# High halves of q and k copied on GpSimd, and the bias of the exponential computed on ScalarE

## The chip, the cores and the metric

The kernel runs on one core of one Trainium2 chip. The metric is the time of one execution on the device in microseconds. A core has five engines that run beside each other, each with its own queue in program order: TensorE (PE in the profile; its weight loads are PEld), VectorE (DVE), ScalarE (ACT), GpSimd (POOL) and SyncE (SP, which here only issues DMAs). An instruction waits at the head of its engine's queue until what it needs is there, and everything behind it on that engine waits too.

## The reference

Attention within clusters, followed by a two-layer network. Each query and key is assigned to the nearest of 16 centroids, and a query attends only to keys of its own cluster:

```
q_assign = argmax(einsum('bhsd,hcd->bhsc', q_n, c_n), axis=-1)     # q_n, c_n: unit length
k_assign = argmax(einsum('bhsd,hcd->bhsc', k_n, c_n), axis=-1)
mask     = q_assign[:, :, :, None] == k_assign[:, :, None, :]
scores   = where(mask, q @ k.T / sqrt(D), -1e9)
attn     = softmax(scores)                                         # with 1e-9 added to the sum
x        = attn @ v                                                # heads joined: 3072 x 512
out      = (s * relu(x @ w_in)**2 + b) @ w_out
```

There are 4 batches, 8 heads, 768 positions, 64 values a head; w_in is 512 x 2048 and w_out 2048 x 512, all float32.

## The kernel before, in words

Every float32 factor of a large product is split in two float16 parts, a high half (the rounded value) and a low half (the rest), and three of the four products of halves are summed.

**Units and steps.** The attention is cut into 192 units, one for each batch, third of the positions, pair of heads, tile of 128 queries and head. The main loop (L699) has one iteration i for each unit. In it stand the scores of unit i (L455: four matmuls of 384 columns into a PSUM tile `sc`, of which there are two), the row maximum on VectorE (`maxima`, L464, which writes the negated maximum into column 0 of a small tile `ssm`), and the exponential (`exps`): L471 computes the bias, maximum times scale plus 14 ln 2, into column 1 of `ssm`, and L474 is the exponential on ScalarE, which reads `sc` and writes `p`. Then `high` (L119: `ph`, the high half of `p`, on ScalarE), `low` (L497: the low half on GpSimd, and L499: a DMA transpose of both halves into `PT`), and four units later `values` (L516 to L518: `PT` times v into `px`, in a single PSUM bank that is shared with small products; L524 to L528 divide by the sums on VectorE).

**The network.** 21 iterations behind the scores runs the network, in 192 steps as well, each with one 128-wide slice of the hidden layer for 256 rows: L574 (12 matmuls into `h`, one bank), L581 (relu on ScalarE, `r`), L583 and L584 (squares, `g` and `r`), L589 (the low half of `g` on GpSimd) and L601 (6 matmuls into `acc`). L609 and L610 scale and write out 256 rows after every 16 steps.

**The weights.** Each of 32 weight tiles is loaded (`wst`), converted on ScalarE (L203, L205, L216), VectorE (L209, L210) and GpSimd (L223), and, when the largest values of all are known, split in halves (L267 on ScalarE, L269 on VectorE). This fills the first iterations.

**The preparation of k and q.** `prep_k` runs 16 times (batch and pair of heads), `prep_q` 24 times (batch, third of the positions, four heads). Both load a block (`kn`, `qn`), find its largest value, scale it and split it: L185 writes the high half on ScalarE and L187 the low half on VectorE. Both build two operands for the scores. For k, `ka` holds the high and the low half side by side, and `kb` the high half and, beside it, a code of the cluster; for q, `qa` holds the low and the high half and `qb` the high half and the code. So the high half stands in both: L325 copies it from `ka` to `kb`, 768 values a partition, and L375 from `qb` to `qa`, 512 values a partition, both on VectorE. The DMA transposes L329 (`KA`) and L379 (`QA`) follow. From `KA` and `QA` TensorE computes the products with the centroids (`pk`, `pq`), VectorE turns them into the code (L288 to L294), and L342 and L392 transpose `kb` and `qb` into `KB` and `QB`. After the first batch there is one `kb` buffer: the copy into it waits until the preceding `KB` transpose has read it. The preparation of a block of q is begun 10 iterations before the first unit that uses it.

**What sets the order.** The program text is not the order of the queues. A scheduler orders every queue from the dependencies and from its own estimates of times; the helpers `behind` and `first_of_all` and the list `last_split` (the last instruction that wrote a half) only bound it at the start. So a change of three lines can reorder all queues.

Of the kernel before, what the change touches and what calls it, by code (L numbers as in the profile page):

```python
# [10 lines left out]
F32 = mybir.dt.float32  # L11
I32 = mybir.dt.int32
U32 = mybir.dt.uint32
AF = mybir.ActivationFunctionType
ALU = mybir.AluOpType
# [3 lines left out]
P = 128  # L19
# [7 lines left out]
def tile_cluster_attention_mlp(ctx, tc, q, k, v, cent, w_in, w_out, s_in, b_in, out):  # L27
# [12 lines left out]
    V = nc.vector  # L40
    G = nc.gpsimd
    A = nc.scalar
# [13 lines left out]
    def const(shape, dt, name):  # L56
        return cp.tile(shape, dt, tag=name, name=name)
# [17 lines left out]
    last_split = [None, None]  # L75
# [97 lines left out]
    bias = []  # L173
# [4 lines left out]
    def split(hi, lo, src, f, early):  # L178
        if early:
            A.activation(src, src, AF.Copy, scale=f)  # L180
            last_split[1] = A.activation(hi, src, AF.Copy)
            yield
            G.tensor_tensor(lo, src, hi, op=ALU.subtract)
        else:
            last_split[1] = A.activation(hi, src, AF.Copy, scale=f)  # L185
            yield
            V.scalar_tensor_tensor(lo, src, f, hi, op0=ALU.mult, op1=ALU.subtract)  # L187

    def fetch(p):
        ft = p // 2  # L190
# [110 lines left out]
    def prep_k(b, hp):  # L301
        kb = kb_kept
        if b == 0 and hp > 0:
            kb = sb.tile([P, 2 * T, P], F16, tag="big", name=f"kb_{hp}", bufs=BIGN).rearrange("p (h t) (e d) -> p h t e d", h=2, e=2)
# [6 lines left out]
        sm = [KSM[b][:, e, hp : hp + 1] for e in range(4)]  # L311
# [8 lines left out]
        if b == 0 and hp > 0:  # L320
            ka = sb.tile([P, 2 * T, P], F16, tag="big", name=f"ka_{hp}", bufs=BIGN).rearrange("p (h t) (e d) -> p h t e d", h=2, e=2)
        else:
            ka = sb.tile([P, 2, T, 2, D], F16, tag="big", name=f"ka_{n}", bufs=BIGN)
        yield from split(ka[:, :, :, 0, :], ka[:, :, :, 1, :], kn, sm[2], False)
        last_split[0] = V.tensor_copy(kb[:, :, :, 0, :], ka[:, :, :, 0, :])  # L325
        KA = sb.tile([P, 2 * T, P], F16, tag="KA", name=f"KA_{n}", bufs=5)
        KB = sb.tile([P, 2 * T, P], F16, tag="KB", name=f"KB_{n}", bufs=5)
        KS[(b, hp)] = (KA, KB)
# [15 lines left out]
    def prep_q(b, c, hq):  # L344
# [8 lines left out]
        sm = sb.tile([P, 4, 2], F32, tag="qsm", name=f"qsm_{n}", bufs=3)  # L353
# [6 lines left out]
        f = sm[:, 2, :]  # L360
# [4 lines left out]
        qa = sb.tile([P, 2 * T * P], F16, tag="big", name=f"qa_{n}", bufs=BIGN)[:, : nh * CT * 2 * D].rearrange("p (h t e d) -> p h t e d", h=nh, t=CT, e=2)  # L365
        qb = sb.tile([P, 2 * T * P], F16, tag="big", name=f"qb_{n}", bufs=BIGN)[:, : nh * CT * 2 * D].rearrange("p (h t e d) -> p h t e d", h=nh, t=CT, e=2)
        both = []
        for j in range(2):
            hs = slice(2 * j, 2 * j + 2)
            both.append(split(qb[:, hs, :, 0, :], qa[:, hs, :, 0, :], qn[:, hs], sm[:, 2, j : j + 1], b + c == 0))  # L370
        for z in zip(*both):
            yield
        for z in both:
            next(z, None)
        V.tensor_copy(qa[:, :, :, 1, :], qb[:, :, :, 0, :])  # L375
        QA = sb.tile([P, nh * CT, P], F16, tag="QA", name=f"QA_{n}", bufs=2)
        QB = sb.tile([P, nh * CT, P], F16, tag="QB", name=f"QB_{n}", bufs=2)
        QS[(b, c, hq)] = (QA, QB, sm)
# [55 lines left out]
                    yield  # L434


    LIFT = 14.0 * math.log(2.0)
    units = [(b, c, hp, t, h) for b in range(B) for c in range(NCH) for hp in range(NP) for t in range(CT) for h in range(2)]
    NU = len(units)
    U = {}  # L440
# [25 lines left out]
    def exps(i):  # L466
        j = i % 4
        sm = SM[i // 4]
        bi = sm[:, 1, j : j + 1]
        u = U[i]  # L470
        V.tensor_scalar(bi, sm[:, 0, j : j + 1], u["scale"], LIFT, op0=ALU.mult, op1=ALU.add)  # L471
        p = sb.tile([P, S], F32, tag="big", name=f"p_{i}", bufs=BIGN)
        total = {"accum_out": sm[:, 2, j : j + 1]} if i < RAW else {}
        last_exp[0] = A.activation(p.rearrange("p (a b) -> p a b", a=2), u["sc"], AF.Exp, bias=bi, scale=u["scale"], **total)  # L474
        u["p"] = p
# [284 lines left out]
```

## Time and profile before

| | |
|---|---|
| median of 3 runs | 1006.37 us (1002.96 to 1007.54) |
| the profiled execution | 1002.93 us |
| its span, first to last instruction | 1001.3 us |
| mean granted TensorE clock in the span | 0.932 of full speed |
| VectorE in L325, L375 and L471 | 15.6, 21.4 and 38.2 us |
| GpSimd's largest group, L497 | 310.3 us in 184 instructions |
| ScalarE's largest group, L474 | 188.4 us in 192 instructions |

How to read the lines below: a group of instructions has its line in the kernel, engine, operation, tile written <- tiles read, sizes and count, then its busy time in all, the mean of one in ns, and the idle time of the engine just before them with what ended it. The busy time of an engine counts overlapping instructions once. The "chain that ended last" is followed back from the last instruction, at each step to what released it or to its predecessor on the engine; its pieces are start, length, and what ran. A line "A <- B: total, times, longest" is the time for which A's engine sat idle until B was done.

### The profile page before, as it was taken

The page shows a single profiled execution, that of the slowest core. Times are in us where ns is not written, and L with a number is a line of the kernel's source. Part 1 is how long each engine was busy: PE and PEld are TensorE (multiplying, and loading weights), DVE is VectorE, ACT ScalarE, POOL GpSimd, SP SyncE. Part 2 cuts the span into 40 slices and gives each one's busy share as a digit, 9 for nine tenths or more (in the row PEclk, how much of TensorE's full clock was granted, in tenths as well). Part 3 has the DMA queues.
Part 4 walks back from the last instruction along what each step waited for, and adds up shares of the span by engine and source line. Part 5 has one row for each costly group of instructions (what it writes and reads, how often), then busy time and mean ns, then how long its engine had stood idle before and what let it go on. Part 6 is the DMA issues. An engine that isn't in the chain of part 4 may idle for free.

```text
span 1001.3 us, 22497 instructions
## 1 busy us (share of the span) xinstructions
PE 845.3 (84%) x8625; PEld 584.2 (58%) x8625; DVE 692.5 (69%) x1707; ACT 675.5 (67%) x1224; POOL 524.9 (52%) x502
## 2 busy tenths in 40 slices
PE   1568436977989899998899999997888998999997
PEld 1346224644566666665566776665666666767764
DVE  6797978889687756768877657687877665574100
ACT  3577666766477777766577877765777775778553
POOL 1225754555255666555466656643566664666422
PEclk9966656999999999999899999998999999999999
DMA  7875986686686976799898679987878776979300
GB/s 186 199 199 171 236 203 117 117 188 116 130 152 134 174 133 117 143 204 173 171 154 155 144 126 170 180 163 159 156 146 169 128 125 129 151 120 160 47 22 22
DMA packets 450299, 147.36 MB, mean 147 GB/s; under 512 B 417936, under 2 KB 446608, under 8 KB 450192
## 3 DMA queue, kind: packets, MB, share of 16 engines
q1 hardware_dynamic: 450192, 145.93, 74.8%
q8 instruction: 67, 1.10, 0.4%
q14 instruction: 40, 0.33, 0.1%
HBM read 35.69 MB, written 6.29 MB: 42 GB/s over the span
## 4 chain that ended last, share of the span: by engine, by line
PE 43%; DVE 19%; DMA 17%; ACT 8%; issue 5%; POOL 3%; SPq 1%; POOLq 0%; DVEq 0%; ACTq 0%
PE h L574 15%; PE acc L601 14%; PE sc L455 6%; DVE ssm L464 4%; DMA PT<-ph 3%; DMA QB<-qb 3%; DMA qn<-in_q_dram 2%; ACT p L474 2%; PE px L516 2%; PE px L518 2%; PE px L517 2%; DMA wst<-in_moe_w_out_dram 2%; DMA KB<-kb 2%; DMA kn<-in_k_dram 2%; POOL ph L497 2%
## 5 line engine op out<-in xcount | busy, mean ns | idle before, releaser
L497 POOL TENSOR_TENSOR ph<-p,ph 128x768 f16<-128x768 f32 x184 | 310.3, 1687 | 225.3 <-ACT ph L119 173.1
L574 PE MATMUL h<-x,wis 128*128 128x256 f16 x2304 | 295.7, 277 | 7.2 <-ACT r L581 2.9
L601 PE MATMUL acc<-wos,g 128*128 128x512 f16 x1152 | 297.4, 380 | 4.0 <-POOL g L589 3.6
L574 PEld LDWEIGHTS <-wis 128*128 128x128 f16 x2304 | 225.2, 99 | 66.0 <-issue 7.7
L474 ACT ACTIVATE p<-sc,ssm,qsm 128x768 f32<-128x768 f32 x192 | 188.4, 981 | 63.0 <-DVE ssm L471 37.2
L589 POOL TENSOR_TENSOR g<-r,g 128x256 f16<-128x256 f32 x192 | 137.2, 715 | 128.2 <-ACT r L584 117.7
L464 DVE TENSOR_REDUCE ssm<-sc 128x1 f32<-128x768 f32 x192 | 181.3, 949 | 24.9 <-PE sc L455 24.8
L581 ACT ACTIVATE r<-h,cf 128x256 f32<-128x256 f32 x192 | 90.0, 469 | 126.0 <-PE h L574 94.5
L601 PEld LDWEIGHTS <-g 128*128 128x128 f16 x1152 | 104.2, 98 | 86.1 <-POOL g L589 7.6
L119 ACT ACTIVATE ph<-p 128x768 f16<-128x768 f32 x174 | 144.8, 832 | 13.0 <-DMA PT<-ph 9.0
L516 PE MATMUL px<-vh,PT 128*128 128x65 f16 x1104 | 122.0, 198 | 22.7 <-DVE qsm L98 7.4
L455 PE MATMUL sc<-KA,QA 128*128 128x384 f16 x384 | 104.2, 351 | 32.9 <-ACT p L474 29.6
L517 PE MATMUL px<-vl,PT 128*128 128x64 f16 x1104 | 122.1, 195 | 0.0
L518 PE MATMUL px<-vh,PT 128*128 128x65 f16 x1104 | 121.6, 196 | 0.0
L517 PEld LDWEIGHTS <-PT 128*128 128x128 f16 x1104 | 105.3, 101 | 24.7 <-issue 16.4
L516 PEld LDWEIGHTS <-PT 128*128 128x128 f16 x1104 | 105.4, 100 | 23.3 <-issue 14.5
L455 PE MATMUL sc<-KB,QB 128*128 128x384 f16 x384 | 102.5, 352 | 17.9 <-DMA QB<-qb 16.1
L518 PEld LDWEIGHTS <-PT 128*128 128x128 f16 x1104 | 105.3, 100 | 3.1
L583 ACT ACTIVATE g<-r 128x256 f16<-128x256 f32 x192 | 79.4, 413 | 3.9
L584 ACT ACTIVATE r<-r 128x256 f32<-128x256 f32 x192 | 79.0, 412 | 3.6
L455 PEld LDWEIGHTS <-QA 128*128 128x128 f16 x384 | 37.2, 103 | 62.4 <-issue 37.4
L455 PEld LDWEIGHTS <-QB 128*128 128x128 f16 x384 | 38.4, 104 | 50.0 <-DMA QB<-qb 22.3
(152 smaller groups left out, 1031.8 us busy)
## 6 DMA issues: line engine op xcount, KB each, us to landing
wst<-in_moe_w_in_dram SPq DMA_DIRECT2D x16, 512.0 KB, 4.5
wst<-in_moe_w_out_dram SPq DMA_DIRECT2D x16, 512.0 KB, 4.0
kn<-in_k_dram SPq DMA_DIRECT2D x16, 384.0 KB, 3.8
qn<-in_q_dram SPq DMA_DIRECT2D x24, 256.0 KB, 3.8
vn<-in_v_dram SPq DMA_DIRECT2D x16, 384.0 KB, 4.1
out_dram<-o SPq DMA_DIRECT2D x12, 512.0 KB, 4.1
PT<-ph SPq DMA_TRANSPOSE x184, 4.0
x<-xn SPq DMA_TRANSPOSE x48, 2.8
```

Of the source, the lines that this page charges most:

```text
L119: A.activation(dst, src, AF.Copy)
L455: last_score[0] = nc.tensor.matmul(sc[:, e, :HALF], X[:, col, :], y[:, h * S + e * HALF : h * S + (e + 1) * HALF], start=st, stop=not st)
L464: last_max[0] = V.tensor_reduce(SM[i // 4][:, 0, j : j + 1], U[i]["sc"], axis=AX.XY, op=ALU.max, negate=True)
L474: last_exp[0] = A.activation(p.rearrange("p (a b) -> p a b", a=2), u["sc"], AF.Exp, bias=bi, scale=u["scale"], **total)
L497: G.tensor_tensor(u["ph"][:, 1, :], u["p"], u["ph"][:, 0, :], op=ALU.subtract)
L516: nc.tensor.matmul(o1, PT[:, kt, :], vh[:, h, kt, : D + 1], start=(kt == 0), stop=False)
L517: nc.tensor.matmul(o, PT[:, kt, :], vl[:, h, kt, :], start=False, stop=False)
L518: nc.tensor.matmul(o1, PT[:, T + kt, :], vh[:, h, kt, : D + 1], start=False, stop=(kt == T - 1))
L574: nc.tensor.matmul(ph[:, :CW], WSP[ft][0][:, wl, kt, :], XS[(b, c, kt)][:, :, xl, :], start=(i == 0), stop=(i == len(terms) - 1))
L581: A.activation(r, ph[:, :CW], AF.Relu, scale=MS[(b, c)][0])
L589: G.tensor_tensor(g[:, 1, :], r, g[:, 0, :], op=ALU.subtract)
L601: nc.tensor.matmul(acc[:, t, :], g[:, gl, rows], WSP[ft][1][:, wl, :], start=(ft == 0 and gl + wl == 0), stop=(ft == NF - 1 and gl == 1))
```

## The change

Three things. The copies L325 and L375 become GpSimd's. The bias of the exponential becomes an activation (Identity, with scale and bias read from memory) on ScalarE, in the queue that also holds the exponential; its constant is a tile `lift`, written once by GpSimd. And at the start, where the copy of k set `last_split[0]`, the low half of a split now sets it.

```
--- before.py
+++ after.py
@@ -184,7 +184,7 @@
         else:
             last_split[1] = A.activation(hi, src, AF.Copy, scale=f)
             yield
-            V.scalar_tensor_tensor(lo, src, f, hi, op0=ALU.mult, op1=ALU.subtract)
+            last_split[0] = V.scalar_tensor_tensor(lo, src, f, hi, op0=ALU.mult, op1=ALU.subtract)
 
     def fetch(p):
         ft = p // 2
@@ -322,7 +322,7 @@
         else:
             ka = sb.tile([P, 2, T, 2, D], F16, tag="big", name=f"ka_{n}", bufs=BIGN)
         yield from split(ka[:, :, :, 0, :], ka[:, :, :, 1, :], kn, sm[2], False)
-        last_split[0] = V.tensor_copy(kb[:, :, :, 0, :], ka[:, :, :, 0, :])
+        G.tensor_copy(kb[:, :, :, 0, :], ka[:, :, :, 0, :])
         KA = sb.tile([P, 2 * T, P], F16, tag="KA", name=f"KA_{n}", bufs=5)
         KB = sb.tile([P, 2 * T, P], F16, tag="KB", name=f"KB_{n}", bufs=5)
         KS[(b, hp)] = (KA, KB)
@@ -372,7 +372,7 @@
             yield
         for z in both:
             next(z, None)
-        V.tensor_copy(qa[:, :, :, 1, :], qb[:, :, :, 0, :])
+        G.tensor_copy(qa[:, :, :, 1, :], qb[:, :, :, 0, :])
         QA = sb.tile([P, nh * CT, P], F16, tag="QA", name=f"QA_{n}", bufs=2)
         QB = sb.tile([P, nh * CT, P], F16, tag="QB", name=f"QB_{n}", bufs=2)
         QS[(b, c, hq)] = (QA, QB, sm)
@@ -434,7 +434,8 @@
                     yield
 
 
-    LIFT = 14.0 * math.log(2.0)
+    lift = const([P, 1], F32, "lift")
+    G.memset(lift, 14.0 * math.log(2.0))
     units = [(b, c, hp, t, h) for b in range(B) for c in range(NCH) for hp in range(NP) for t in range(CT) for h in range(2)]
     NU = len(units)
     U = {}
@@ -468,7 +469,7 @@
         sm = SM[i // 4]
         bi = sm[:, 1, j : j + 1]
         u = U[i]
-        V.tensor_scalar(bi, sm[:, 0, j : j + 1], u["scale"], LIFT, op0=ALU.mult, op1=ALU.add)
+        A.activation(bi, sm[:, 0, j : j + 1], AF.Identity, scale=u["scale"], bias=lift)
         p = sb.tile([P, S], F32, tag="big", name=f"p_{i}", bufs=BIGN)
         total = {"accum_out": sm[:, 2, j : j + 1]} if i < RAW else {}
         last_exp[0] = A.activation(p.rearrange("p (a b) -> p a b", a=2), u["sc"], AF.Exp, bias=bi, scale=u["scale"], **total)
```

Lines behind L437 have moved by one: L472 below is the bias, L475 the exponential, L498 `ph` on GpSimd, L582, L584 and L585 are `r`, `g` and `r`, and L590 is `g` on GpSimd.

The scheduler orders the queues anew. SP's queue at the start, before: the first transposes of k (KA) and of the centroids (cT), loads, and the first transpose of q (QA).

```order
L329 DMA_TRANSPOSE KA_0_0_192<-ka_0_0_158 128x12x128
L329 DMA_TRANSPOSE KA_0_1_203<-ka_1_169 128x12x128
L160 DMA_TRANSPOSE cT_126<-cnat_120 128x3x128
L82 DMA vn_0_0_248<-in_v_dram 128x2x384
L125 DMA sv_250<-in_moe_s_dram 128x1
L125 DMA bv_252<-in_moe_b_dram 128x1
L379 DMA_TRANSPOSE QA_0_0_0_198<-qa_0_0_0_184 128x8x128
L82 DMA wst_0_255<-in_moe_w_in_dram 128x4x256
L82 DMA wst_1_258<-in_moe_w_out_dram 128x1024
L82 DMA wst_2_266<-in_moe_w_in_dram 128x4x256
L342 DMA_TRANSPOSE KB_0_0_193<-kb_131 128x12x128
```

And the same place with the change:

```order
L329 DMA_TRANSPOSE KA_0_0_194<-ka_0_0_160 128x12x128
L329 DMA_TRANSPOSE KA_0_1_205<-ka_1_171 128x12x128
L82 DMA vn_0_0_250<-in_v_dram 128x2x384
L125 DMA sv_252<-in_moe_s_dram 128x1
L125 DMA bv_254<-in_moe_b_dram 128x1
L82 DMA wst_0_257<-in_moe_w_in_dram 128x4x256
L160 DMA_TRANSPOSE cT_126<-cnat_120 128x3x128
L82 DMA wst_1_260<-in_moe_w_out_dram 128x1024
L82 DMA wst_2_268<-in_moe_w_in_dram 128x4x256
L379 DMA_TRANSPOSE QA_0_0_0_200<-qa_0_0_0_186 128x8x128
L342 DMA_TRANSPOSE KB_0_0_195<-kb_131 128x12x128
```

The transpose into QA has moved behind the three weight loads `wst`, and cT behind the first of them.

GpSimd's queue about unit 57, where the block of q for batch 1, second third, first four heads is prepared, before:

```order
L497 TENSOR_TENSOR ph_56_4460<-p_56_4418,ph_56_4460 128x768
L589 TENSOR_TENSOR g_0_2_2_4348<-r_0_2_2_4346,g_0_2_2_4348 128x256
L497 TENSOR_TENSOR ph_57_4550<-p_57_4464,ph_57_4550 128x768
L589 TENSOR_TENSOR g_0_2_3_4435<-r_0_2_3_4433,g_0_2_3_4435 128x256
L497 TENSOR_TENSOR ph_58_4595<-p_58_4554,ph_58_4595 128x768
L589 TENSOR_TENSOR g_0_2_4_4481<-r_0_2_4_4479,g_0_2_4_4481 128x256
```

With the change:

```order
L498 TENSOR_TENSOR ph_56_4462<-p_56_4420,ph_56_4462 128x768
L590 TENSOR_TENSOR g_0_2_3_4437<-r_0_2_3_4435,g_0_2_3_4437 128x256
L498 TENSOR_TENSOR ph_57_4552<-p_57_4466,ph_57_4552 128x768
L375 COPY qa_1_1_0_4537<-qb_1_1_0_4538 128x8x64
L498 TENSOR_TENSOR ph_58_4597<-p_58_4556,ph_58_4597 128x768
L590 TENSOR_TENSOR g_0_2_4_4483<-r_0_2_4_4481,g_0_2_4_4483 128x256
```

The copy into `qa_1_1_0` stands between the low halves of units 57 and 58.

ScalarE's queue at the same place, before:

```order
L474 ACTIVATE p_57_4464<-sc_57_4449,ssm_56_4415,qsm_1_0_1_3832 128x768
L584 ACTIVATE r_0_2_2_4346<-r_0_2_2_4346 128x256
L581 ACTIVATE r_0_2_3_4433<-h_0_2_3_4420,cf_0_2_4198 128x256
L185 ACTIVATE qb_1_1_0_4536<-qn_1_1_0_4313,qsm_1_1_0_4395 128x4x64 x2
L583 ACTIVATE g_0_2_3_4435<-r_0_2_3_4433 128x256
L119 ACTIVATE ph_57_4550<-p_57_4464 128x768
L474 ACTIVATE p_58_4554<-sc_58_4539,ssm_56_4415,qsm_1_0_1_3832 128x768
```

With the change:

```order
L475 ACTIVATE p_57_4466<-sc_57_4451,ssm_56_4417,qsm_1_0_1_3834 128x768
L584 ACTIVATE g_0_2_3_4437<-r_0_2_3_4435 128x256
L585 ACTIVATE r_0_2_3_4435<-r_0_2_3_4435 128x256
L472 ACTIVATE ssm_56_4417<-ssm_56_4417,lift_132,qsm_1_0_1_3834 128x1
L185 ACTIVATE qb_1_1_0_4538<-qn_1_1_0_4315,qsm_1_1_0_4397 128x4x64 x2
L119 ACTIVATE ph_57_4552<-p_57_4466 128x768
L475 ACTIVATE p_58_4556<-sc_58_4541,ssm_56_4417,qsm_1_0_1_3834 128x768
```

The bias for unit 58 (into `ssm_56`, the small tile of units 56 to 59) stands ahead of the high halves of q and of unit 57's `ph`, three rows before the exponential that reads it. Over the whole queue 165 of the 192 biases have other work between them and their exponential.

More of the change, by code (lines that the diff above doesn't have):

```diff
@@ L186, in split @@
             yield
-            V.scalar_tensor_tensor(lo, src, f, hi, op0=ALU.mult, op1=ALU.subtract)
+            last_split[0] = V.scalar_tensor_tensor(lo, src, f, hi, op0=ALU.mult, op1=ALU.subtract)
     def fetch(p):
@@ L324, in prep_k @@
         yield from split(ka[:, :, :, 0, :], ka[:, :, :, 1, :], kn, sm[2], False)
-        last_split[0] = V.tensor_copy(kb[:, :, :, 0, :], ka[:, :, :, 0, :])
+        G.tensor_copy(kb[:, :, :, 0, :], ka[:, :, :, 0, :])
         KA = sb.tile([P, 2 * T, P], F16, tag="KA", name=f"KA_{n}", bufs=5)
@@ L374, in prep_q @@
             next(z, None)
-        V.tensor_copy(qa[:, :, :, 1, :], qb[:, :, :, 0, :])
+        G.tensor_copy(qa[:, :, :, 1, :], qb[:, :, :, 0, :])
         QA = sb.tile([P, nh * CT, P], F16, tag="QA", name=f"QA_{n}", bufs=2)
@@ L434, in prep_v @@
                     yield
-    LIFT = 14.0 * math.log(2.0)
+    lift = const([P, 1], F32, "lift")
+    G.memset(lift, 14.0 * math.log(2.0))
     units = [(b, c, hp, t, h) for b in range(B) for c in range(NCH) for hp in range(NP) for t in range(CT) for h in range(2)]
@@ L470, in exps @@
         u = U[i]
-        V.tensor_scalar(bi, sm[:, 0, j : j + 1], u["scale"], LIFT, op0=ALU.mult, op1=ALU.add)
+        A.activation(bi, sm[:, 0, j : j + 1], AF.Identity, scale=u["scale"], bias=lift)
         p = sb.tile([P, S], F32, tag="big", name=f"p_{i}", bufs=BIGN)
```

## The prediction, made before the changed kernel was run

> **What bounds the kernel now.** I read the page first (busy times, chain), then the busy time of each engine by stage, then the waits of TensorE.
>
> ```profile
> span 1001.3 us, 22497 instructions
> ...
> PE 845.3 (84%) x8625; PEld 584.2 (58%) x8625; DVE 692.5 (69%) x1707; ACT 675.5 (67%) x1224; POOL 524.9 (52%) x502
> ...
> PE 43%; DVE 19%; DMA 17%; ACT 8%; issue 5%; POOL 3%; SPq 1%; POOLq 0%; DVEq 0%; ACTq 0%
> ```
>
> TensorE (PE) is the busiest engine and holds 43% of the chain that ended last. VectorE (DVE), which the change relieves, holds 19%, ScalarE (ACT) 8% and GpSimd (POOL) 3%. The work goes to the two engines that count least. But the averages hide stages:
>
> ```profile
> core 0: us, PE busy (x) PEld busy (x) DVE busy (x) ACT busy (x) POOL busy (x), PEclk, DMA share, GB/s
> 0.00:200.00 200.00, 111.73 (x943) 78.66 (x944) 168.93 (x406) 127.48 (x229) 91.13 (x99) 0.75 0.75 178
> 200.00:300.00 100.00, 83.69 (x818) 53.23 (x816) 81.41 (x189) 62.52 (x111) 46.51 (x40) 0.95 0.75 147
> 300.00:950.00 650.00, 604.37 (x6563) 422.56 (x6561) 439.39 (x1110) 463.24 (x835) 375.28 (x347) 0.98 0.81 148
> ```
>
> The columns are the stretch, its length, and the busy time and instructions of each engine. In the first 300 us, in which the weights are converted, VectorE is busy for 168.9 + 81.4 = 250.3 us, 83%: it is the engine to relieve. From 300 to 950 us TensorE is busy for 604.4 of 650 us, 93%. Whatever the other engines gain there, no more than the 45.6 us in which TensorE is idle can be won, and only where they cause the idling:
>
> ```profile
> PE sc L455 <- DMA QB<-qb: 11.1, 10, 2.7
> PE sc L455 <- ACT p L474: 6.0, 7, 1.3
> ...
> PE h L574 <- ACT r L581: 2.6, 6, 0.7
> ```
>
> These are waits of TensorE from 300 to 950 us (total, times, longest). The largest is for QB, the end of the preparation of q in which one of the moved copies stands; the other two are for ScalarE, which gets more to do.
>
> **Part 1: the bias of the exponential.** What is removed, and two of the places where it stood on the chain:
>
> ```profile
> L471 DVE TENSOR_SCALAR ssm<-ssm,qsm 128x1 f32<-128x1 f32 x192 | 38.2, 206 | 1.6
> ```
>
> ```profile
> 54.90 0.20 DVE ssm L471
> ...
> 785.83 0.13 DVE ssm L471
> ```
>
> These two are the first and the last of 38 pieces of the chain, 5.5 us in all. VectorE loses 192 x 0.206 = 38.2 us, but only 5.5 us of that was on the path. ScalarE gains 192 activations of one element with scale and bias read from memory. No such row exists; the nearest are:
>
> ```profile
> L474 ACT ACTIVATE p<-sc,ssm,qsm 128x768 f32<-128x768 f32 x192 | 188.4, 981 | 63.0 <-DVE ssm L471 37.2 <-DMA PT<-ph 7.2 <-PE h L574 5.0
> L119 ACT ACTIVATE ph<-p 128x768 f16<-128x768 f32 x174 | 144.8, 832 | 13.0 <-DMA PT<-ph 9.0 <-DMA QA<-qa 1.7 <-DMA QB<-qb 1.2
> ...
> L583 ACT ACTIVATE g<-r 128x256 f16<-128x256 f32 x192 | 79.4, 413 | 3.9
> ```
>
> From L583 and L119, (832 - 413) / 512 = 0.82 ns an element, so 204 ns without any element. The exponential has the same two operands from memory as the new bias, and 981 - 768 x 0.82 = 351 ns. The price lies between 0.20 and 0.35 us; I take 0.35, the row with the same operands. That is 67 us more on ScalarE, which then stands at about 74%. On the chain an activation takes less, since the next starts before it ends:
>
> ```profile
> 553.10 0.73 ACT ph L119
> ```
>
> 0.73 against 0.83 us: 0.10 less. So the 38 places cost 38 x 0.25 = 9.5 us instead of 5.5 us: **+4.0 us** (with 0.10 each, 3.8 us: -1.7). Elsewhere the bias lies beside TensorE. That cover is gone where a bias at the head of ScalarE's queue waits for its maximum; behind it stand the copies to ph, and the activations r and g on which GpSimd and then TensorE wait. This is the second rival.
>
> **Part 2: the copies.** The groups removed, and the nearest rows for a copy on GpSimd:
>
> ```profile
> L375 DVE COPY qa<-qb 128x512 f16<-128x512 f16 x24 | 21.4, 893 | 0.0
> ...
> L325 DVE COPY kb<-ka 128x768 f16<-128x768 f16 x16 | 15.6, 978 | 7.7 <-DMA KB<-kb 7.5
> ```
>
> ```profile
> L497 POOL TENSOR_TENSOR ph<-p,ph 128x768 f16<-128x768 f32 x184 | 310.3, 1687 | 225.3 <-ACT ph L119 173.1 <-issue 10.6 <-PE px L518 9.6
> ...
> L113 POOL CAST identb<-ident 128x128 bf16<-128x128 f32 x1 | 0.3, 305 | 0.0
> L108 POOL MEMSET ones<- 128x128 bf16 x1 | 0.2, 205 | 0.0
> ```
>
> ```profile
> L106 POOL MEMSET rev<- 128x1 f32 x16 | 0.6, 98 | 0.3 <-POOLq L746 0.3
> ```
>
> VectorE loses 21.4 + 15.6 = 37.0 us. For GpSimd the dearest neighbour is the subtraction with two inputs, 1687 / 768 = 2.2 ns an element; the cheapest is the memset, which reads nothing: 205 ns for 128 elements and 98 ns for one, so 0.84 ns an element. The cast, one input and one output as the copy has, took 305 ns for 128; less the 0.1 us of the memset of one element that is 1.6 ns an element, so 0.9 us for q (512) and 1.3 us for k (768). Taking the cast, 24 x 0.9 + 16 x 1.3 = 42 us; by the dearest row 24 x 1.13 + 16 x 1.69 = 54 us, by the cheapest 24 x 0.53 + 16 x 0.74 = 25 us. GpSimd goes from 52% to about 57% and has idle time to hide it; what counts is where a copy stands in its queue. On the chain:
>
> ```profile
> 219.12 1.71 DVE kb L325
> ...
> 287.99 1.40 DVE qa L375
> ...
> 355.71 1.65 DVE qa L375
> 467.57 1.57 DVE kb L325
> ...
> 631.83 1.65 DVE qa L375
> ...
> 781.99 1.65 DVE qa L375
> ```
>
> Those are the six longest of 15 pieces: the copies for k hold 6.4 us of the chain (6 pieces), those for q 8.4 us (9 pieces).
>
> The k copy is needed late, for KB, so off VectorE nearly all of it goes. Where it waited for the preceding KB to leave the buffer (the 7.5 us in its row), GpSimd now waits instead, with ph behind it. I take **-5 us** (from 0 to -6.4).
>
> The q copy is needed at once, for QA. VectorE did it behind the two low halves (L187). In the changed order GpSimd does it behind a whole ph, and that ph behind ScalarE's copy, which itself stands behind the high halves. From the high halves on, that is 0.83 + 1.69 + 0.9 = 3.4 us. Before, it was two L187 and the copy:
>
> ```profile
> L187 DVE SCALAR_TENSOR_TENSOR qa<-qn,qsm,qb 128x256 f16<-128x256 f32 x44 | 38.0, 900 | 4.9 <-DMA PT<-ph 4.8 <-issue 0.2
> ```
>
> 2 x 0.90 + 0.89 = 2.7 us. Three pieces of 1.65 us above are about as long as one ph of GpSimd (1.69), which suggests that VectorE was held up there by that ph; on GpSimd the copy comes after it all the same. So the 8.4 us are replaced by 9 x 0.9 = 8.1 us: **0 us** (from -8.4, if the low halves are what is late, to 9 x 0.7 = +6.3).
>
> ```profile
> L375 DVE COPY qa<-qb x24: 277/754/1739, 16.5 to 882.6; 128x512 f16<-128x512 f16 x24
> ```
>
> The same copy took 277 ns at least, 754 in the middle and 1739 at most. The Trainium skill (SBUF — State Buffer, "SBUF: two separate sides") says that VectorE in its two-port modes and GpSimd share one pair of ports, locked for a whole instruction, so that the other blocks. The spread of this row agrees. By that rule the copy never beats GpSimd's ph on either engine and the q term is 0; without it the copy would simply be a slow instruction removed, the term -8.4 us and the sum some 8 us lower.
>
> **Part 3: what is moved.** The order of every queue is newly made. At the start the first QA goes behind three weight loads in SP's queue:
>
> ```profile
> 18.40 1.25 SPq L379 DMA_TRANSPOSE QA<-qa  x1
> 19.70 0.58 SPq L82 DMA_DIRECT2D wst<-in_moe_w_in_dram  x1
> 20.32 0.52 SPq L82 DMA_DIRECT2D wst<-in_moe_w_out_dram  x1
> 20.88 0.46 SPq L82 DMA_DIRECT2D wst<-in_moe_w_in_dram  x1
> ```
>
> Their issue takes 0.58 + 0.52 + 0.46 = **+1.6 us** before the first scores; if it also had to wait for one load to land (4.5 us by the page), 6 us. VectorE converts weights meanwhile, so 0 is the other end. Then the relief of VectorE's queue beyond the places on the chain: before 300 us the rows that go are
>
> ```profile
> 0.00:200.00 200.00, 5.96 (x30) 0.75 0.75 178
> 200.00:300.00 100.00, 3.16 (x16) 0.95 0.75 147
> ```
>
> for the bias, 9.1 us, and 10.6 us of copies by the same view, 19.7 us; 8.9 us of that is on the chain and counted. Of the other 10.8 us a queue that is 83% busy passes on something between nothing and all; I take half, **-5 us**. After 300 us I take nothing, since TensorE is at 93%.
>
> **Sum.** +4.0 - 5 + 0 + 1.6 - 5 = -4.4 us. Against the profiled run of 1002.9 us (span 1001.3 and 1.6 around it) that is 998.5. The median of the runs shown is 1006.4, 3.4 above the profiled one, so a median comes out at **1002 us**.
>
> **Rivals.** *Nothing arrives.* TensorE's 93% after 300 us and the bank of h, read by ScalarE before the next h, keep the pace, and the start gives back what it gains: 1006 us. For it speaks that 38 us of the bias had only 5.5 on the chain; against it VectorE's 83% before 300 us.
>
> *ScalarE's queue becomes the wait (slower).* In 165 of the 192 places the bias now stands with other work between it and its exponential. Today ScalarE waits 37.2 us, 24 times, for the bias of VectorE (in L474's row), with the exponential at the head. If that wait comes as often at the bias, with r and g behind it, and half of it, 18.6 us, reaches TensorE through h and acc, then the sum is +18.6 - 4.4 = +14 us: 1020 us. It decides from the point at which r comes later than TensorE can run ahead with one bank of h; so far that costs 2.6 us in 6 waits, which speaks against it. The Trainium skill (ScalarE: Activation LUTs, "Rules for kernel authors") tells to keep multiply and add on VectorE; it names this side, and the rows agree in so far as 0.206 us becomes 0.35.
>
> *The q path gets shorter.* VectorE is free sooner for the maximum and for the one-hot of q; most QB transposes stand earlier in SP's new order. If TensorE's 11.1 us of waits for QB go in full, and the weight stage gives all of the 10.8 us instead of half: -4.4 - 11.1 - 5.4 = -21 us: 985 us. Against it, QA comes later by 0.7 us per chunk as worked out above.
>
> *The change does not do what it says:* the bias could need another function table on each use. ScalarE's queue in the new order holds the same two table loads as before, so this gets no chance.
>
> **Chances and range.** Forecast, 996 to 1008 us: 0.45; nothing arrives: 0.13; ScalarE's queue: 0.24; shorter q path: 0.18. Half a per cent, 5 us, is about what a measurement of this kernel can tell from no change. Of the forecast 0.22 lies under 1001.4 us. Faster is 0.22 + 0.18 = 0.40, within 0.5% 0.23 + 0.13 = 0.36, slower 0.24. The lower bounds of the terms sum to -1.7 - 6.4 - 8.4 - 10.8 = -27, the upper ones to 4 + 6.3 + 6 = +16; not all fall together, so the range is 984 to 1019 us, which leaves out about half of the slower rival and the far end of the fast one.
>
> **What would show it.** Right: L471 gone from VectorE and an activation of about 0.35 us on ScalarE; copies on GpSimd of 0.9 and 1.3 us; ScalarE's busy share at 72 to 74%, VectorE's at 60 to 63%; the first matmul of h some microseconds earlier; 300 to 950 us with TensorE at 92 to 94%. Wrong: waits of ScalarE for the maximum (L464) well above 37 us with r behind them; TensorE's waits for QA or QB above 20 us; copies on GpSimd over 1.7 us; VectorE's other rows stretched by more than they gain.

## The result, and the profile after

| | before | changed |
|---|---|---|
| median, timed together (4 runs each) | 1004.66 us (1000.5 to 1007.54) | 988.80 us (987.78 to 992.24) |
| ratio of the two | | 0.9853, 95% interval 0.9819 to 0.9887 |
| the profiled execution, and its span | 1002.93 us, 1001.3 us | 987.78 us, 986.0 us |
| mean granted TensorE clock, profiled | 0.932 | 0.941 |

The changed kernel is 1.5% faster. From here on line numbers of an experiment are those of its own kernel, and may differ by one to three from the changed kernel's.

The head of the page of the changed kernel, busy time of each engine:

```profile
span 986.0 us, 22497 instructions
...
PE 834.3 (85%) x8625; PEld 580.2 (59%) x8625; DVE 673.0 (68%) x1475; ACT 726.4 (74%) x1416; POOL 550.2 (56%) x543
```

ScalarE stands at 74% and GpSimd at 56%, as worked out. VectorE does not stand at 60 to 63%: 75.2 us of work left it (38.2 + 21.4 + 15.6) and its busy time fell by 19.5 us. The new rows, and some VectorE rows that were not edited, from the groups of instructions of the changed kernel:

```profile
L472 ACT ACTIVATE ssm<-ssm,lift,qsm 128x1 f32<-128x1 f32 x192 | 73.4, 382 | 101.9 <-DVE ssm L465 101.4
...
L291 DVE TENSOR_TENSOR oe_q<-oe_q,rev 128x128 f32<-128x128 f32 x24 | 20.4, 849 | 0.5
...
L375 POOL COPY qa<-qb 128x512 f16<-128x512 f16 x24 | 18.0, 750 | 0.0
...
L325 POOL COPY kb<-ka 128x768 f16<-128x768 f16 x16 | 15.7, 982 | 32.9 <-DMA KB<-kb 23.9 <-ACT ka L185 8.9
...
L69 DVE TENSOR_SCALAR qsm<-qsm 128x2 int32<-128x2 int32 x24 | 14.0, 583 | 0.5
...
L362 DVE TENSOR_TENSOR qsm<-qsm,ksm 128x2 f32<-128x2 f32 x24 | 10.7, 444 | 0.6
```

The bias takes 382 ns, the copies 750 and 982 ns. ScalarE now sits idle at the bias for 101.4 us until the maximum is there, where it sat 37.2 us at the exponential. VectorE's three rows took 14.0, 5.7 and 4.3 us before; they cost 21.1 us more, though nothing in them was changed. In all, the work that stayed on VectorE takes 55.7 us more (75.2 less 19.5).

Where the time went, by stages of the changed kernel:

```profile
core 0: us, PE busy (x) PEld busy (x) DVE busy (x) ACT busy (x) POOL busy (x), PEclk, DMA share, GB/s
0.00:200.00 200.00, 106.72 (x908) 75.78 (x909) 172.55 (x362) 131.84 (x251) 93.60 (x107) 0.74 0.68 174
200.00:300.00 100.00, 86.86 (x852) 56.11 (x850) 81.12 (x171) 70.93 (x134) 53.55 (x49) 0.97 0.80 150
300.00:950.00 650.00, 610.25 (x6665) 428.44 (x6663) 417.95 (x942) 508.73 (x999) 394.98 (x377) 1.00 0.73 149
```

By 300 us TensorE had 1760 matmuls behind it, where it had 1761 before (943 + 818): the start gained nothing. From 300 to 950 us it did 6665 where it had done 6563, in 5.9 us more of busy time and at a granted clock of 1.00 where it had 0.98. So the whole gain lies behind 300 us, and a part of it is clock. TensorE's waits in that stretch, in the changed kernel:

```profile
PE h L575 <- ACT r L582: 12.2, 10, 3.1
PE sc L456 <- ACT p L475: 6.0, 6, 1.8
PE sc L456 <- DMA QB<-qb: 5.8, 7, 2.0
```

The wait for QB halved (11.1 before), that for the relu grew (2.6 before). The waits for VectorE, spread over a dozen rows of at most 4 us each, fell most; the account below adds them up.

### The profile page after: what moved, and what is told of

Read it like the earlier page. It is cut to its first block, busy times and chain, and to the rows that moved or that the text cites. A ratio compares the mean times of both kernels' runs of the same rounds, so it can differ in the third digit from the quotient of the medians.

```text
span 986.0 us, 22497 instructions
## 1 busy us (share of the span) xinstructions
PE 834.3 (85%) x8625; PEld 580.2 (59%) x8625; DVE 673.0 (68%) x1475; ACT 726.4 (74%) x1416; POOL 550.2 (56%) x543
## 5 line engine op out<-in xcount | busy, mean ns | idle before, releaser
L498 POOL TENSOR_TENSOR ph<-p,ph 128x768 f16<-128x768 f32 x184 | 308.6, 1677 | 170.7 <-ACT ph L119 135.8
L575 PE MATMUL h<-x,wis 128*128 128x256 f16 x2304 | 292.0, 275 | 17.3 <-ACT r L582 12.2
L590 POOL TENSOR_TENSOR g<-r,g 128x256 f16<-128x256 f32 x192 | 133.3, 695 | 139.7 <-ACT r L585 129.8
L475 ACT ACTIVATE p<-sc,ssm,qsm 128x768 f32<-128x768 f32 x192 | 188.1, 980 | 3.9 <-DMA PT<-ph 1.8
L119 ACT ACTIVATE ph<-p 128x768 f16<-128x768 f32 x174 | 144.8, 832 | 11.1 <-DMA PT<-ph 10.8
L472 ACT ACTIVATE ssm<-ssm,lift,qsm 128x1 f32<-128x1 f32 x192 | 73.4, 382 | 101.9 <-DVE ssm L465 101.4
L517 PE MATMUL px<-vh,PT 128*128 128x65 f16 x1104 | 119.9, 196 | 14.5 <-DVE ksm L98 5.2
L582 ACT ACTIVATE r<-h,cf 128x256 f32<-128x256 f32 x192 | 89.1, 464 | 55.0 <-PE h L575 50.8
L518 PE MATMUL px<-vl,PT 128*128 128x64 f16 x1104 | 119.9, 193 | 0.0
L519 PE MATMUL px<-vh,PT 128*128 128x65 f16 x1104 | 119.9, 194 | 0.0
L456 PE MATMUL sc<-KA,QA 128*128 128x384 f16 x384 | 101.1, 343 | 20.2 <-ACT p L475 16.9
L518 PEld LDWEIGHTS <-PT 128*128 128x128 f16 x1104 | 103.6, 100 | 21.2 <-issue 12.8
L517 PEld LDWEIGHTS <-PT 128*128 128x128 f16 x1104 | 103.9, 98 | 17.5 <-issue 9.1
L456 PE MATMUL sc<-KB,QB 128*128 128x384 f16 x384 | 100.2, 345 | 7.8 <-DMA QB<-qb 7.7
L519 PEld LDWEIGHTS <-PT 128*128 128x128 f16 x1104 | 103.6, 98 | 3.0
L584 ACT ACTIVATE g<-r 128x256 f16<-128x256 f32 x192 | 79.5, 414 | 3.8
L585 ACT ACTIVATE r<-r 128x256 f32<-128x256 f32 x192 | 79.1, 412 | 3.3
L525 DVE TENSOR_SCALAR ssm<-px 128x2 f32<-128x2 f32 x92 | 14.2, 155 | 88.3 <-PE px L519 88.2
```

What stands on the lines that cost most here:

```text
L119: A.activation(dst, src, AF.Copy)
L456: last_score[0] = nc.tensor.matmul(sc[:, e, :HALF], X[:, col, :], y[:, h * S + e * HALF : h * S + (e + 1) * HALF], start=st, stop=not st)
L498: G.tensor_tensor(u["ph"][:, 1, :], u["p"], u["ph"][:, 0, :], op=ALU.subtract)
L517: nc.tensor.matmul(o1, PT[:, kt, :], vh[:, h, kt, : D + 1], start=(kt == 0), stop=False)
L518: nc.tensor.matmul(o, PT[:, kt, :], vl[:, h, kt, :], start=False, stop=False)
L519: nc.tensor.matmul(o1, PT[:, T + kt, :], vh[:, h, kt, : D + 1], start=False, stop=(kt == T - 1))
```

## What the clock has to do with it

In the kernel before, TensorE's clock falls to half for some microseconds in five places between 300 and 930 us. One of them, as the windows of the kernel before show it (stretch, length, busy time and matmuls, granted clock):

```profile
core 0: us, PE busy (x), PEclk, DMA share, GB/s
650.00:652.00 2.00, 1.29 (x7) 1.00 0.95 135
652.00:654.00 2.00, 0.79 (x4) 0.87 1.43 264
654.00:656.00 2.00, 2.00 (x19) 0.50 0.95 256
656.00:658.00 2.00, 2.00 (x28) 0.78 0.21 72
658.00:660.00 2.00, 2.00 (x23) 1.00 0.18 37
```

and the timeline of TensorE in the same place (start, duration, line, operation; in brackets the idle time ahead and what ended it):

```profile
649.94 0.33 PE L455 MATMUL sc<-KA,QA 128*128 128x384 f16 x1
...
653.21 0.59 PE L455 MATMUL sc<-KB,QB 128*128 128x384 f16 x2 [1.92 <-DMA QB<-qb]
653.60 0.84 PE L455 MATMUL sc<-KA,QA 128*128 128x384 f16 x2
```

One wait of 1.92 us for QB, and the matmuls behind it run at half clock for 3.4 us: another 1.7 us lost. In windows of 1 us each, all such stretches between 300 and 930 us in all 14 profiled kernels lose 1.7 us or a multiple of it (3.4 us at half clock, or two or three of these in a row). A wait of about the same length in the changed kernel (1.81 us, from 485.9 us on) passed without it:

```profile
486.00:488.00 2.00, 0.31 (x2) 1.00 0.33 62
488.00:490.00 2.00, 2.00 (x20) 1.00 0.87 197
```

The Trainium skill (TensorE: Matmul & The Clock Gate, "Why this matters for your kernels") warns of idle gaps above about 3 us between bursts of matmuls. Here one of 1.92 us was followed by the half clock, and three longer ones were not: one of 3.30 us in the kernel before and two in the changed kernel, of 3.05 and 3.12 us. One of these:

```profile
475.18 1.03 PE L575 MATMUL h<-x,wis 128*128 128x256 f16 x8 [3.05 <-ACT r L582]
```

So the length of a single wait does not decide it. The starts of the half clock show what does. In windows of 0.2 us, the five places of the kernel before begin at 339.5, 479.4, 653.5, 687.6 and 834.4 us; their distances are 41, 51, 10 and 43 times 3.413 us. The clock changes on a grid of this step, and so it does in every profiled execution with two places or more, each with a grid of its own. Three stretches of the grid in the kernel before, the first with the wait of 1.92 us:

```profile
650.08:653.49 3.41, 1.49 (x9) 1.00 1.03 193
653.49:656.90 3.41, 3.41 (x25) 0.50 1.03 225
656.90:660.32 3.42, 3.42 (x43) 1.00 0.21 41
```

and two in the changed kernel, which share the wait of 3.05 us:

```profile
470.58:473.99 3.41, 1.55 (x18) 1.00 1.49 207
473.99:477.41 3.42, 2.23 (x34) 1.00 0.82 248
```

Idle were 1.92 us of the first stretch, and 1.86 and 1.19 us of the last two. Between 300 and 930 us of the 14 executions, a stretch at full clock with 1.95 us idle or more was followed by the half clock in 47 of 47 cases, one with less than 1.46 us in none of 2337, and one between these in 16 of 78. Short waits add up: in x3 below, both half-clock places stand behind three waits of 0.67 to 0.76 us each. In the changed kernel five stretches with 1.73 to 1.92 us idle passed at full clock, in the kernel before one (1.75 us). Since the grid lies differently in each execution, part of what the clock brings is luck.

## Experiments: each part by itself

Four kernels, each the kernel before with a part of the change, and its queues as the scheduler then orders them.

**e1, the bias alone**

```
-    LIFT = 14.0 * math.log(2.0)
+    lift = const([P, 1], F32, "lift")
+    G.memset(lift, 14.0 * math.log(2.0))
...
-        V.tensor_scalar(bi, sm[:, 0, j : j + 1], u["scale"], LIFT, op0=ALU.mult, op1=ALU.add)
+        A.activation(bi, sm[:, 0, j : j + 1], AF.Identity, scale=u["scale"], bias=lift)
```

> Only the bias moves to ScalarE; both copies stay on VectorE. Relief theory (the gain of 15 us comes from less work on VectorE where batches' k, q and v are prepared): the bias is 38 of the 75 us taken off VectorE, so about half the gain, ratio to before 0.992 (0.988 to 0.996). Path theory (only what stood on the chain counts: 5.5 us of bias leave, 38 places at 0.28 us = 10.6 us come): ratio 1.005. Order theory (the gain is a by-product of the newly made queues): anything between 0.985 and 1.015, and the ratios of the parts do not multiply to 0.985.

**e2, the copies alone** (both copies, and the line of `last_split`)

```
-            V.scalar_tensor_tensor(lo, src, f, hi, op0=ALU.mult, op1=ALU.subtract)
+            last_split[0] = V.scalar_tensor_tensor(lo, src, f, hi, op0=ALU.mult, op1=ALU.subtract)
...
-        last_split[0] = V.tensor_copy(kb[:, :, :, 0, :], ka[:, :, :, 0, :])
+        G.tensor_copy(kb[:, :, :, 0, :], ka[:, :, :, 0, :])
...
-        V.tensor_copy(qa[:, :, :, 1, :], qb[:, :, :, 0, :])
+        G.tensor_copy(qa[:, :, :, 1, :], qb[:, :, :, 0, :])
```

> Both copies on GpSimd, the bias stays on VectorE. Relief theory: 37 of 75 us, about half, ratio 0.992 (0.988 to 0.996). Path theory: the copies held 14.8 us of the chain, so nearly the whole gain, 0.985 to 0.988. Order theory: anything between 0.985 and 1.015.

**e3, the copy of k alone** (e2 without its last edit)

> Only the k copy moves (15.6 us of VectorE, 6.4 us of the chain). Relief theory: 0.997. Path theory: 0.994. By the prediction's own term (-5 us): 0.995. Order theory: anything between 0.985 and 1.015.

**e4, the copy of q alone** (only the last edit of e2)

> Only the q copy moves (21.4 us of VectorE, 8.4 us of the chain). Relief theory: 0.995. Path theory, if the copy on GpSimd is not late for QA: 0.992. By the prediction's own term (0 us, since GpSimd does it behind a whole ph): 1.000. Order theory: anything between 0.985 and 1.015.

Timed beside 29 runs of the kernel before (median 1003.45 us):

| | median us | ratio to before | 95% interval |
|---|---|---|---|
| e1 biases | 1004.96 | 1.0017 | 0.9994 to 1.0040 |
| e2 copies | 1008.25 | 1.0048 | 1.0024 to 1.0072 |
| e3 copy of k | 1015.90 | 1.0107 | 1.0074 to 1.0140 |
| e4 copy of q | 1002.74 | 0.9995 | 0.9972 to 1.0018 |

Neither part brings anything alone; the product of e1 and e2 is 1.0065, and the whole is 0.9853. Taken at its word this says that the parts need each other. But each of the four kernels also has queues of its own: against the kernel before, 6143 of 8577 TensorE instructions of the changed kernel stand at another place in the queue, in e1 5354 and in e2 6934. What was measured is a part together with an order.

## Experiments: engine and order apart

To part the two, the order was taken out of the scheduler's hands. At the end of the kernel each engine's instructions are chained in the order of a list, by edges that fix the order of issue and ask for no semaphore:

```
+    for k in ORDER:                       # the scheduler's list of the one or the other kernel
+        x = traced[k]
+        y = prev.get(str(x.engine))
+        if y is not None:
+            tc.add_manual_dep(x, y, mybir.DependencyInfo(mybir.DependencyClass.NoSync, mybir.DependencyReason.DATA), reason="order")
+        prev[str(x.engine)] = x.name
```

With the list of the kernel before, all unmoved instructions of a changed kernel stand on every engine exactly as before, and only the moved ones change their queue. No kernel was timed chained in its own list, as a control of the chaining itself; the nearest to it is x3 below, which differs from the changed kernel by six copies and is as fast.

**x1: the changed kernel, in the order of before**

> The changed kernel's instructions, each on its new engine (192 biases on ScalarE, 40 copies on GpSimd), but every engine's queue pinned to the order of the kernel before; a moved instruction stands in its new queue where the scheduler's list of before has it. Nothing of the computation is changed. Engine theory (the gain comes from VectorE's 75 us of work going to engines with room): 0.983 to 0.990 of before, as the whole change. Order theory (the gain comes from the new order of the queues that the scheduler made): 0.997 to 1.008, and the step of the network that begins at 759 us in before begins within 4 us of it, not 10.7 us earlier. If the start's delay belongs to the copies on GpSimd, the first h comes 5 to 10 us late here too; if to the order, it comes at 148.5 us as before.

**x2: the kernel before (with the line of `last_split` changed), in the order of the changed kernel**

> The kernel before with every instruction on its old engine (biases and copies on VectorE), but every engine's queue pinned to the order that the changed kernel has; the 232 instructions stand in VectorE's queue where the changed kernel's list has them. Order theory: 0.982 to 0.992 of before, as the whole change. Engine theory: 0.997 to 1.006. If the two parts need each other (a new order that VectorE's relief makes possible): 0.995 or more here and 0.995 or more for the new engines in the old order.

**o1: the kernel before with only that line changed, the scheduler free**

```
+            last_split[0] = V.scalar_tensor_tensor(lo, src, f, hi, op0=ALU.mult, op1=ALU.subtract)
...
-        last_split[0] = V.tensor_copy(kb[:, :, :, 0, :], ka[:, :, :, 0, :])
+        V.tensor_copy(kb[:, :, :, 0, :], ka[:, :, :, 0, :])
```

> The kernel before with only the line of the change that makes the scheduler place the early work behind another instruction (the split's second half in place of k's copy); no instruction changes its engine. Order theory: orders alone move this kernel's time by up to 1% either way, so anything from 0.990 to 1.012 fits, and a ratio outside 0.997 to 1.003 bears it out. Engine theory: 0.998 to 1.003.

| | order of before | order of changed |
|---|---|---|
| all on the old engines | 1 (the kernel before) | x2: 1.0208 (1.0174 to 1.0242) |
| all on the new engines | x1: 0.9924 (0.9897 to 0.9951) | the change: 0.9853 (0.9819 to 0.9887) |

o1, with no instruction on another engine, is 1.0080 (1.0051 to 1.0108).

Neither theory holds alone. The engines by themselves, in the old order, bring 0.8%. The new order with the old engines loses 2.1%, and with the new engines gains 0.7%: it suits the engines for which it was made. And o1 shows how far a mere hint to the scheduler moves this kernel. The four results of e1 to e4 therefore say little of their parts: they lie within what orders alone do (+0.8% and +2.1%).

**x3: the changed kernel in its own order, with the first batch's six copies on VectorE**

```
-        G.tensor_copy(kb[:, :, :, 0, :], ka[:, :, :, 0, :])
+        (V if b == 0 else G).tensor_copy(kb[:, :, :, 0, :], ka[:, :, :, 0, :])
...
-        G.tensor_copy(qa[:, :, :, 1, :], qb[:, :, :, 0, :])
+        (V if b + c == 0 else G).tensor_copy(qa[:, :, :, 1, :], qb[:, :, :, 0, :])
```

> The changed kernel in its own pinned order, with the six copies of the first batch's start (four of k, two of q) back on VectorE. If the 8.6 us by which the first h comes late are the copies' time on GpSimd, the first h comes 4 to 9 us earlier than the changed kernel's 157.1 us; that carries to the end if the later stretches are bound by TensorE (980 to 985 us), and is lost by step 24, as the delay itself was, if the weights' split sets that stretch (987 to 990 us). If the delay is of the order alone, the first h stays at 155 to 159 us.

x3 took 987.34 us, 0.9826 (0.9796 to 0.9856): faster than the kernel before, and not to be told from the changed one. The first matmul of `h` is the first of the two starts in the row of its line (behind the durations: least, median, most). In the kernel before:

```profile
L574 PE MATMUL h<-x,wis x2304: 269/273/421, 148.5 to 992.6; 128*128 128x256 f16 x192
```

in the changed kernel:

```profile
L575 PE MATMUL h<-x,wis x2304: 269/273/421, 157.1 to 977.5; 128*128 128x256 f16 x192
```

in x1:

```profile
L577 PE MATMUL h<-x,wis x2304: 268/273/422, 149.8 to 982.9; 128*128 128x256 f16 x192
```

in x2:

```profile
L576 PE MATMUL h<-x,wis x2304: 269/273/422, 157.6 to 1015.6; 128*128 128x256 f16 x192
```

in x3:

```profile
L577 PE MATMUL h<-x,wis x2304: 268/273/422, 156.9 to 975.1; 128*128 128x256 f16 x192
```

The delay of 8.6 us goes with the order (157.6 in x2, 149.8 in x1) and not with the copies' engine (156.9 in x3). By 300 us it has cost nothing: TensorE did other matmuls in the meantime, 1760 as shown above.

## Experiments: which part, in a fixed order

**y1: e1's edit, in the order of before**

> Only the biases are on ScalarE; every queue stands in the order of the kernel before, so only the engine of 192 instructions differs from it. The whole change in this order gave 0.9924. If VectorE's relief gives that gain, the biases bring about two thirds of it by their share of the time that leaves VectorE (48 of 75 us): 0.993 to 0.997. If the copies bring it: 0.999 to 1.003. By the prediction's own sum the bias on the chain costs 4.0 us: 1.002 to 1.006.

**y2: e2's edits, in the order of before**

> Only the copies of k and q are on GpSimd; every queue stands in the order of the kernel before. Relief theory by time (27 of 75 us): 0.996 to 0.999. If the copies bring the whole gain: 0.991 to 0.995. If they pay for their GpSimd time while the biases bring the gain: 1.000 to 1.005. Where the two parts only add, this ratio times that of the biases alone in the same order is 0.9924.

**z1: e1's edit and o1's, in the order of the changed kernel**

> Biases on ScalarE, copies on VectorE, every queue in the order that the changed kernel has. In this order the whole change is 0.9853 and none of it 1.0208. If what the new order needs is the biases out of VectorE's queue, where they stand behind work that comes late: 0.984 to 0.992. If it needs the copies out of VectorE's queue: 1.012 to 1.021. If it is VectorE's relief by time, two thirds of the way: 0.994 to 1.000.

| moved | order of before | order of changed |
|---|---|---|
| nothing | 1 | 1.0208 (1.0174 to 1.0242) |
| biases | y1: 0.9963 (0.9940 to 0.9986) | z1: 0.9894 (0.9860 to 0.9928) |
| copies | y2: 1.0006 (0.9983 to 1.0028) | not run |
| both | 0.9924 (0.9897 to 0.9951) | 0.9853 (0.9819 to 0.9887) |

Each of the three lies in a range that was expected of it: y1 as the larger part of the relief, y2 as copies that pay for their time on GpSimd, z1 as an order that needs the biases out of VectorE's queue. The biases bring 0.4% in the old order and 3.1% in the new one. The copies bring nothing alone; on top of the biases they bring 0.4% in both orders, but those intervals overlap, so this is likely and not shown. One way through the table: biases 0.4, copies 0.4, order 0.7%, together the 1.5%.

How the copies pay is seen in y2, whose queues differ from the kernel before only by them. TensorE's wait for `g`, whose low half GpSimd computes, from 300 to 930 us:

```profile
PE acc L603 <- POOL g L591: 12.4, 8, 3.6
```

It was 0.8 us in the kernel before and is 7.0 in x1, but 1.8 in the changed kernel: in the old order the copies hold up `g`, in the new one they hardly do.

The biases' two gains point to what the new order needs: the exponential must not depend on VectorE's queue a second time. In x2 the row of the bias agrees (who waited for it on VectorE: total and times):

```profile
L473 DVE TENSOR_SCALAR ssm<-ssm,qsm x192: 192/204/215, 38.4 to 946.2; 128x1 f32<-128x1 f32 x192
...
  ACT p L476: 49.5, 24
```

49.5 us of waits of the exponential for the bias, 37.2 in the kernel before. These 12.3 us are not the whole of the 3.1% (31 us) between x2 and z1. Of x2's loss some 7 us lie outside the stretch from 300 to 930 us: by 300 us TensorE had 1679 matmuls behind it, where it had 1761. Which of the reordered places makes it was not traced further.

## Experiment: is the wait on ScalarE harmful?

**w1: the changed kernel in its own order, but each bias directly ahead of its exponential in ScalarE's queue** (in the list of the order, 192 places moved; no other line changed)

> The changed kernel in its own pinned order, but each of the 192 biases moved in ScalarE's queue to the place directly ahead of its exponential (in the changed kernel 165 have other work between, most often the relu r and the two squares behind it). This tests the prediction's rival that ScalarE's queue becomes the wait. If that wait (ScalarE idle at a bias until VectorE's maximum, 101.4 us before the 192 biases, with r queued behind) costs what TensorE waits for r (h for r: 12.2 us from 300 us on, 2.6 in the kernel before), the time falls by up to 10 us: 0.975 to 0.981 of before, and that row falls to 3 to 5 us. If it is hidden: 0.983 to 0.988 and the row changes without the time. If the bias directly ahead of the exponential lengthens the way from the maximum to the next scores, as the prediction's chain term has it: 0.988 to 0.996.

w1 took 995.17 us, 0.9915 (0.9884 to 0.9946): 0.6% above the changed kernel, in the range of the third branch. The two intervals just touch. The bias in w1, with the idle time of ScalarE before it, and TensorE's waits from 300 to 950 us in w1:

```profile
L474 ACT ACTIVATE ssm<-ssm,lift,qsm x192: 370/372/398, 38.0 to 922.0; 128x1 f32<-128x1 f32 x192
its engine sat idle before it (us, times) until:
  DVE ssm L467: 24.7, 16
```

```profile
PE h L577 <- ACT r L584: 11.4, 4, 3.7
PE sc L458 <- ACT p L477: 10.7, 16, 2.4
PE sc L458 <- DMA QB<-qb: 6.4, 6, 1.9
```

ScalarE's idle time at the bias fell from 101.4 to 24.7 us, and the time did not follow. TensorE's wait for the relu stayed at 11 us, so it is not made by the biases ahead of it. It comes mostly with the new order: in x2, where every bias is on VectorE, it stands (from 300 to 930 us) at

```profile
PE h L576 <- ACT r L583: 9.2, 9, 2.6
```

and in z1 at 10.5 us, while with the biases on ScalarE in the old order it is 4.2 us (x1) and 5.9 us (y1).

What grew in w1 is the wait of the scores for the exponential, from 6.0 us (6 times) to 10.7 (16 times): now the bias's 0.37 us stand directly ahead of every exponential. In the changed kernel ScalarE waits early and is done with the bias when it is needed. But other waits shrank by as much. TensorE's idle time is 39.4 us in w1 and 39.6 in the changed kernel (the account below); what makes the profiled execution longer is half clock, 17.1 us against 1.7. Of the 17.1 us 3.4 stand behind a wait for the exponential and 8.5 behind three waits for the relu. So the cost of the place directly ahead of the exponential is suggested by w1 and not shown.

## The account: waits and clock

So a wait of TensorE is worth its length and, where a stretch of the grid gets too much idle time, 1.7 us more. Both, summed over the 630 windows from 300 to 930 us of each profiled execution:

```
                                    TensorE idle   lost to half clock   sum    span
before                                   45.7            11.9           57.6   1001.3
changed                                  39.6             1.7           41.3    986.0
x1  new engines, order of before         41.2             8.5           49.7    991.7
x2  old engines, order of changed        59.6            13.7           73.3   1024.2
x3  first copies back on VectorE         35.2             3.4           38.6    983.8
y1  biases only, order of before         46.9            10.2           57.1    998.6
y2  copies only, order of before         51.0            10.2           61.2   1005.9
z1  biases only, order of changed        39.4             8.5           47.9    989.6
w1  bias next to its exponential         39.4            17.1           56.5    998.4
```

Before to changed, the sum falls by 16.3 us and the span by 15.3 us: the result lies in these two. In the other rows sum and span move together within 2.2 us, but for x2, whose other 7 us lie before 300 us or behind 930 us. 6.1 us are waits, 10.2 us clock. TensorE's waits in the same stretch, added up by the engine that ended them (us):

| | VectorE | ScalarE | DMA | GpSimd |
|---|---|---|---|---|
| before | 22.4 | 8.6 | 12.8 | 0.8 |
| changed | 12.2 | 18.2 | 6.4 | 1.8 |
| x1 | 11.0 | 10.1 | 11.7 | 7.0 |
| x2 | 24.0 | 20.2 | 13.9 | 2.5 |
| y1 | 20.3 | 15.3 | 9.7 | 0.8 |
| y2 | 17.8 | 9.0 | 12.0 | 12.4 |
| z1 | 14.5 | 15.0 | 7.7 | 1.4 |
| w1 | 8.6 | 22.1 | 6.9 | 1.1 |

The waits for VectorE fell by 10.2 us and those for DMA by 6.4; those for ScalarE grew by 9.6. With both moves the waits for VectorE are about halved in either order (x1 and the changed kernel); those for ScalarE grow with the new order even on the old engines (x2). The profiled execution of the changed kernel was a lucky one in this: its mean clock is 0.941, that of the four timed runs 0.9385 on average, that of 42 runs of the kernel before 0.9334. The difference of 0.005 over 990 us is 5 us, so over many executions nearer 5 than 10 of the 15 us are clock (an estimate: the mean clock is that of the whole span). What the order adds with the new engines, x1 to changed, is the least sure: in the two profiles 1.6 us of it are waits and 6.8 us clock, and by the mean clocks (0.9355 over x1's six runs) some 3 of the 7 us are clock. The same holds for w1: its profiled execution, 1000.15 us, is 5 us above its median, and over its seven runs its clock is 0.934, which gives 4 of the 6 us between it and the changed kernel by the same estimate.

## Why the prediction came out as it did

The forecast was 1002 us against 1006.4, 4.4 us less; the result is 988.8 us against 1004.7, 15.9 us less. That lies outside the forecast's own 996 to 1008 us and inside the range of 984 to 1019 us, beside the faster rival (985 us), and for other reasons than that rival gave. That it fell inside the range is partly luck, since some 5 to 10 us of it are clock, which no term held. Point by point:

- **The step that failed** is in part 3 and in the first part: "After 300 us I take nothing, since TensorE is at 93%". All of the gain lies there. The 45.6 us of idle time were rightly named as all that can be won by waits, but two things were left out: waits can cost half clock besides (11.9 us in the kernel before, though its 0.98 stood in the quoted row), and 7% of idle time is enough for 6 us of gain. The term taken as nothing was VectorE's relief in this stage: TensorE's waits for VectorE fell there from 22.4 to 12.2 us, those for ScalarE took 9.6 us back, and the half clock fell from 11.9 to 1.7 us in the profiled execution.
- **The price of the bias** was right (0.35 taken, 0.382 measured), its term not. +4.0 us was to come of its place on the chain. Alone in the old order it gains 3.7 us (0.9963). Whether the mechanism costs anything once the bias stands directly ahead of the exponential, w1 leaves open; in the changed kernel it stands earlier in 165 of 192 places, and these places had been seen and were counted only as a danger. (A slip beside it: 192 x 0.206 is 39.6 us; 38.2 is the busy time of the row.)
- **The copies** were priced at 0.9 and 1.3 us and took 0.75 and 0.98. The k term of -5 and the q term of 0 met 0.6 us of loss for both alone (1.0006) and some 4 us of gain beside the biases: the sum is about right in the second case, for a reason that the chain had not shown: whether the copies on GpSimd hold up `g` depends on the order (12.4 us of TensorE's waits in y2, 1.8 in the changed kernel).
- **The start**: neither +1.6 us nor -5 us. The first `h` came 8.6 us later, not earlier, and by 300 us TensorE stood where it had stood.
- **VectorE's relief** was put in the wrong stage: -5 us before 300 us, where nothing was gained, and nothing after. Its busy time was overrated as well: it fell by 19.5 us, not by 75, since its other rows took longer.
- **The second rival's trigger came, its effect did not.** ScalarE waited 101.4 us for the maximum, well above 37, with `r` behind it, which was named as the sign of a wrong forecast. TensorE's wait for `r` did grow, from 2.6 to 12.2 us, but w1 and x2 show that it does not come of this waiting: it stays when the waiting goes, and it is there with the biases on VectorE.
- **The third rival** had the time (985 us), and a part of the cause: the waits for QB fell by 5.3 us, not by 11.1, and the stage of the weights gave nothing.
- **The new order** was treated at SP's start alone. It is worth as much as both moves: 0.7% with the new engines (part of it clock), and 2.1% the other way without them.

## What to carry to other kernels

Where a scheduler orders the queues, a part of a change that is built alone is measured with an order of its own; pin the order before believing that a part helps, hurts, or needs another. An engine that is 93% busy in a stage is no reason to write off the stage: list its waits, short ones that stand close together too, and look at the clock behind them. Moving a small step between a slow producer and a critical consumer to the consumer's engine gained in both fixed orders here (0.4% and 3.1%), though not when the scheduler ordered that part anew (1.0017); whether it has to stand some places ahead of the consumer is open.

## What was not expected of the hardware

The half clock in pieces of 3.4 us, each worth 1.7 us: seven of them in the kernel before between 300 and 930 us (five places, two of them double), one in the changed kernel. They begin on a grid of 3.413 us, after a stretch of it in which TensorE was idle for about 1.5 to 1.9 us or more, so that a wait of 3 us can pass where one of 1.92 us does not. And VectorE's smallest rows: two integers a partition took 236 ns on average before and 583 ns in the changed kernel (L69, 24 times). In the old order the same row took 349 ns with the copies alone, 310 ns with the biases alone and 483 ns with both; in the new order 345 ns with neither, 524 ns with the biases alone, and 374 ns in w1. So order and engines act together; what stretches it stays open.
